# RWKV-7 scan and a four-expert mixture: key and removal vectors turned to channels by loads and VectorE, with one reciprocal of the channel-major decay

## The chip, the cores and the metric

One core of one Trainium2 chip. The metric is the device time of one launch in microseconds: for the kernel before, the median of 3 runs is 1080.28 us (1080.03 to 1081.78). The profiles come from one further execution under the hardware profiler.

## What is computed

A recurrence over 768 steps, for 4 batches and 8 heads with 40 channels each, and behind it a mixture of four two-layer experts on the recurrence's output (3072 rows of 320). All data are fp32.

```python
for t in range(S):                                   # S = 768; state: (B, H, 40, 40)
    y[:, :, t] = einsum('bhd,bhde->bhe', r_t, state)
    Sa = einsum('bhde,bhe->bhd', state, a_t)
    state = state * w_t[:, :, None, :] - einsum('bhd,bhe->bhde', Sa, b_t) + einsum('bhd,bhe->bhde', v_t, k_t)

x = y as (4*768, 8*40);  p = domain_probs / (domain_probs.sum(-1) + 1e-9)
out = sum over e of p[:, e] * (relu(x @ w1[e]) @ w2[e])     # w1: 4 x 320 x 1024, w2: 4 x 1024 x 320
```

The decay w is multiplied up along the steps, per channel. Inside a stretch of steps, the kernel scales k and b by the reciprocal of that running product, and a and r by the product itself; then the stretch is a set of ordinary matrix products.

## The kernel before

**Tiling.** The 768 steps are cut into 12 chunks of L = 64. A chunk of two batches (8 heads each) is a *unit*: 24 units, number u = 2 x chunk + pair of batches. All the work of a unit on the recurrence is in tiles of 128 partitions: either *by tokens* (2 batches x 64 steps on the partitions, 8 heads x 40 channels in the row, 320 elements) or *by channels* (2 heads x 64 places on the partitions, of which 40 carry a channel, 8 pairs x 64 steps in the row, 512 elements).

**One unit on its way.** `within()` (L458) prepares a unit by itself. SP loads the decay in 32-wide pieces as `rawW` (`load_raw`, L264), DVE turns it to channels with two 32x32 stream transposes into G (L475, helper line L286), saves the decay of the last step (gl, L477), sets the first column to zero (G0, L479), and a scan along the row makes the running product (L512; `first` is one in each first column); gl is brought up to the product of all 64 steps (L517). PE turns G back to tokens (pg, L525, four transposes recorded on helper line L113), DVE multiplies by the naturally loaded decay `natW` (gp, L528) and takes the reciprocal of 128x320 (L529). With it DVE makes N = -b/g (n_tok, L556) and K = k/g (k_tok, L561) by tokens, from `natB` and `natK`, and AT from `rawA` (L563, and L565, AG, times G). `VT` and `RT` are the values and receptances by channels, from `rawV` and `rawR`. PE turns N and K to channels (pNT, pKT, `turned()`, L532 to L535), ACT copies them out of PSUM to NT and KT. From these PE makes the scores pc, pfe and pe. POOL then solves a triangular system (`substitute`, Z, L681 and L698), about 22 us a unit; DVE turns the result (Qc, QTc, L709, L710).

`begin_step` is the part that hangs on the state left by the unit two before: prn (PE; with the state), RH (DVE, L760), psat, SX, pxr, RS, then pdy (PE), Y, S+, YG, SG (DVE, L823 to L835). Y, the output, is copied by twelve small SP loads into `xT` (L854), the operand of the mixture.

**The mixture.** For each pair of units and each expert: up-projections `ph` (two PSUM tiles, PE), hs = relu (ACT, L888), five sums of parts of hs on DVE (`a`, L1014), and seven products in the manner of Strassen in place of eight: `p431`, `p75`, `p26` (all shown as `p` in the profile). DVE adds each into the output tile, scaled by the gate (osb: L903, of 320 or of 160 elements). `lead()` lets PE begin the next ph early, before the last matmuls of a scan step. The up-projection weights w1a and w1b come in pieces, three loads each (L365).

**PSUM.** Eight banks: five are handed out in turn under the tag "big" (scan), three under "mm" (ph twice, p431, p75, p26). A bank is given to the next tile only once its last reader is through.

**What sets the order.** PE's order is the program's (`keep_in_program_order`). DVE's is stated in the string VECTOR_ORDER for the first units (the names are `G3.0`, `1/gp3`, ...), with `pin()` beside it for units up to 3; past that the tile scheduler places DVE's instructions by their data and its own costs. SP issues nearly all loads, in one order, which the scheduler makes too; an issue that waits for a tile to come free holds up everything behind it. At most eight of its DMAs are under way at once. Until PADDED = 3 a unit uses other loads; from unit EARLY = 5 on the main loop has its steady order. In the steady state I call *section* s the stretch of about 42.4 us that begins with RH of unit s: it holds the step of unit s and the first half of `within()` of unit s+3.

Of the kernel before, what the change touches and what calls it, by code (L numbers as in the profile page):

```python
# [15 lines left out]

VECTOR_ORDER = """
    Qc1 QTc1 G2.0 G2.1 gl2 G02 scan2 gll2 out1 gp2 1/gp2 N2 K2 AT2 AG2 RTc2.0 RTc2.1 RTc2.2 VTc2.2 blocks2.0
    blocks2.1 M2 M02 Z12 Z22 ET2.0 ET2.1 VC2.0 VC2.1 out2 G3.0 G3.1 gl3 G03 scan3 SX1.1 gll3 SX1.0 VT3 RT3 AT3 AG3
    Y1.1 Y1.0 S+1.0 S+1.1 SG1.0 SG1.1 gp3 1/gp3 N3 K3 out3 VC3.0 VC3.1 Qc2 QTc2 RH2.0 RH2.1 G4.0 G4.1 gl4 G04  # L20
    blocks3.0 blocks3.1 M3 M03 Z13 Z23 ET3.0 ET3.1 out4 SX2.0 SX2.1 scan4 gll4 AT4 AG4 VT4 RT4 Y2.1 Y2.0 S+2.0 YG2
    SG2.0 S+2.1 gp4 SG2.1 1/gp4 N4 K4 out5 VC4.1 VC4.0 sum_w0 Qc3 QTc3 ET4.0 blocks4.0 blocks4.1 ET4.1 M4 M04 Z14
    Z24 RH3.0 RH3.1 G5.0 sum_w1 G5.1 gl5 G05 scan5 gll5 sum_w2 AT5 AG5 out6 SX3.0 SX3.1 sum_w3 VT5 Y3.1 Y3.0 S+3.0
    YG3 SG3.0 S+3.1 gp5 SG3.1 1/gp5 RT5 N5 K5 sum_w4 out7 VC5.1 VC5.0 Qc4 QTc4 ET5.0 blocks5.0 blocks5.1 ET5.1 M5
    M05 Z15 Z25 RH4.0 RH4.1 G6.0 G6.1 gl6 G06 scan6 sum_a4 gll6 sum_w5 sum_w6 AT6 AG6 sum_a0 sum_a1 sum_a2 sum_a3
    SX4.0 SX4.1 sum_w7 VT6 sum_w8 Y4.1 Y4.0 S+4.0 YG4 SG4.0 S+4.1 gp6 SG4.1 1/gp6 RT6 N6 K6 out8 out9 out10 out11
    sum_a5 VC6.1 VC6.0 Qc5 QTc5 out12 out13 ET6.0 blocks6.0 blocks6.1 ET6.1 M6 M06 Z16 Z26 out14 out15 sum_w9 sum_a6
    G7.0 G7.1 gl7 G07 RH5.0 RH5.1 scan7 gll7 sum_a7 sum_a8 sum_a9 AT7 AG7 out16 out17 out18 out19 sum_w10 sum_w11
    SX5.0 SX5.1 sum_w12 sum_w13 sum_w14 sum_a10 sum_a11 out20 sum_a12 out21 sum_a13 VT7 out22 sum_a14 out23 gp7 1/gp7
"""  # L30


# [1 line left out]
def kernel(  # L34
# [42 lines left out]
    P = 128  # L77
# [95 lines left out]
                        base=(2 * j + s) * D - g * P, channel_multiplier=1,  # L173
                    )

    first = const.tile([P, 2 * NJ, L], FP32, name="first")
    nc.gpsimd.memset(first[:], 0.0)
    nc.gpsimd.memset(first[:, :, 0:1], 1.0)


    def kept(name, shape, n, value=0.0, eng=nc.gpsimd, lo=0):
# [19 lines left out]
    for n, a_sum in enumerate(("a1", "a7", "a5", "a2")):  # L201
        t = padded["RV"[n % 2], n // 2] = sb.tile([P, H, 64], FP32, name="padded", tag=a_sum)
        nc.gpsimd.memset(t[:, :, D:64], 0.0)
    raw = {x: kept(f"raw{x}", [P, 2 * NJ, 2 * D], 1, 0.0, nc.vector, D + D - Q) for x in "WARV"}
    k_tok, n_tok = (kept(x, of_64, 2, lo=D) for x in ("k_tok", "n_tok"))

    both = [P, H, D + L]
# [30 lines left out]

    def load(q, names):
        for x in names:  # L240
            q.n[x] = t = sb.tile([P, H, D], FP32, name=f"nat{x}", tag=f"nat{x}", bufs=2 if x in "WV" else 1)
            for i, bb in enumerate(q.b):
                nc.sync.dma_start(
                    out=t[i * L:(i + 1) * L], in_=srcs[x][bb, :, q.c * L:(q.c + 1) * L, :].rearrange("h t e -> t h e"),
                )

    def load_raw(q, names):


        moves = []  # L250
        for x in names:
            q.n["raw" + x] = t = raw[x]()
            heads = srcs[x].rearrange("b h t e -> (b h) t e")[q.b[0] * H:(q.b[1] + 1) * H, q.c * L:(q.c + 1) * L, :]
            heads = heads.rearrange("n (x two) e -> x n (two e)", two=2)
            for r in range(2):
                if x in "RV":

                    sets = ((slice(0, 8, 2), slice(r, 16, 4)), (slice(1, 8, 2), slice(3 - r, 16, 4)))
                else:
                    sets = ((slice(0, 8), slice(r, 16, 2)),)  # L260
                for n, hs in sets:
                    for y, w_ in enumerate((D + Q, 2 * D - Q)):
                        o = slice(64 * r + Q * y, 64 * r + Q * y + Q)
                        moves.append(lambda eng, out=t[o, n, 0:w_], in_=heads[:, hs, Q * y:Q * y + w_]: eng.dma_start(out=out, in_=in_))  # L264
        return moves
# [7 lines left out]
    def part(i):  # L273
        return slice(i * L, (i + 1) * L)
# [119 lines left out]
    def half(s):  # L394
        return slice(64 * s, 64 * s + 64)
# [22 lines left out]
    def tok(x):  # L418
        return lambda j: x[:, 2 * j:2 * j + 2, :].rearrange("p h e -> p (h e)")

    def of_pairs(x, hf, j, i):
        return x[half(hf), j, part(i)]

    def of_slots(x, hf, j, i, n=64):
        return x[64 * hf:64 * hf + n, 4 * i + j, :]
# [36 lines left out]
    def within(q):  # L462
# [3 lines left out]
        def pin(ins, also=False):  # L466
            if q.u <= PADDED or also:
                keep(ins)


        G = sb.tile([P, 2 * NJ * L + 1], FP32, name="G", tag="G", bufs=3)
        q.G = Gv = G[:, 0:2 * NJ * L].rearrange("p (c t) -> p c t", t=L)
        ahead = G[:, 1:2 * NJ * L + 1].rearrange("p (j i t) -> p i j t", i=2, t=L)
        for i in range(2):
            pin(noted(turn_raw(ahead[:, i], n["rawW"][:, NJ * i:NJ * i + NJ, :]), "G", q.u, i), q.u > EARLY + 2)  # L475
        q.gl = sb.tile([P, 2 * NJ, 1], FP32, name="gl", tag="gl", bufs=4)
        ins = nc.vector.tensor_tensor(out=q.gl[:], in0=G[:, L::L][:, :, None], in1=first[:, :, 0:1], op=ALU.mult)  # L477
        pin(noted(ins, "gl", q.u))
        pin(noted(nc.vector.memset(Gv[:, :, 0:1], 0.0), "G0", q.u))  # L479
        q.AT = sb.tile([P, 2 * NJ, L], FP32, name="AT", tag="AT", bufs=2)  # L480

# [24 lines left out]
        if q.u == 1:  # L506
            yield
            VT = turn_rv("V")
            yield
            turn_rv("R")  # L510
            yield
        ins = nc.vector.tensor_tensor_scan(  # L512
            out=G[:, 0:2 * NJ * L], data0=G[:, 0:2 * NJ * L],
            data1=first[:].rearrange("p c i -> p (c i)"), initial=0.0, op0=ALU.mult, op1=ALU.add,
        )
        pin(noted(ins, "scan", q.u))
        ins = nc.vector.tensor_tensor(out=q.gl[:], in0=q.gl[:], in1=Gv[:, :, L - 1:L], op=ALU.mult)  # L517
        noted(ins, "gll", q.u)
        if q.u == 1:
            yield  # L520
        if q.u < 3:
            pin(noted(turn_raw(q.AT[:], n["rawA"][:]), "AT", q.u))
        yield

        pg = turn("pg", tok(Gv), q.u == 2, of_mixture("pg") if q.u == 1 else None)  # L525
        pg = by(pg[:], 64)[:, :, 0:D]
        gp = sb.tile([P, H, D], FP32, name="gp")
        pin(noted(nc.vector.tensor_tensor(out=gp[:], in0=pg, in1=n["W"][:], op=ALU.mult), "gp", q.u))  # L528
        pin(noted(nc.vector.reciprocal(out=gp[:], in_=gp[:]), "1/gp", q.u))  # L529

        yield

        def turned(name, x):
            t = sb.tile([P, NJ, P], FP32, name=name, tag="turned", bufs=3)
            nc.scalar.copy(out=t[:].rearrange("p j t -> p (j t)"), in_=turn("p" + name, tok(x), q.u == 1)[:])  # L535
            return t

        def token_V():
            return n["paddedV"][:, :, 0:D] if q.u < PADDED else n["V"][:]

        def causal_scores(VT):
            pc = quadrants(banks("pc"), 0, BY_TOKENS, L, lambda j, s, i: (
# [6 lines left out]
        def masks(pc):  # L549
# [3 lines left out]
                    pin(ins, q.start)  # L553

        q.K, q.N = k_tok(), n_tok()
        ins = nc.vector.scalar_tensor_tensor(  # L556
            out=q.N[:, :, 0:D], in0=n["B"][:], scalar=-1.0, in1=gp[:], op0=ALU.mult, op1=ALU.mult,
        )
        pin(noted(ins, "N", q.u))
        other = nc.gpsimd if q.u == 1 else nc.vector  # L560
        pin(noted(other.tensor_tensor(out=q.K[:, :, 0:D], in0=n["K"][:], in1=gp[:], op=ALU.mult), "K", q.u))  # L561
        if q.u > 2:
            pin(noted(turn_raw(q.AT[:], n["rawA"][:]), "AT", q.u))  # L563
        at_ij = q.AT[:].rearrange("p (i j) t -> p i j t", i=2)
# [2 lines left out]
        q.VC = VCs()  # L567
        if q.u > 0:
            noted(nc.scalar.copy(out=q.VC[:, :, 0:D], in_=token_V()), "VCv", q.u)
        if q.u >= PADDED:  # L570
            VT = turn_rv()
        yield

        NT = turned("NT", q.N)
        KT = turned("KT", q.K)
        if q.u == 2:
            VT = turn_rv()
        yield
# [1 line left out]
        if q.u == 1 or q.u >= PADDED:  # L580
# [2 lines left out]

        p = banks("pfe")
        pf = quadrants(p, 0, BY_TOKENS, L, lambda j, s, i: (
            s, i ^ s, j, of_slots(q.AT, s, j, i), of_pairs(NT, s, j, i),
        ))
        def copy_F():
            q.F = sb.tile([P, H, L], FP32, name="F", tag="F", bufs=1)
# [6 lines left out]
        if q.apart or q.u == 0:  # L596
            p = banks("pe")
        pe = quadrants(p, NJ * L, BY_TOKENS, L, lambda j, s, i: (
            s, i, j, of_pairs(KT, s, j, i), of_slots(q.AT, s, j, i),
        ))  # L600
        if not q.apart:
            copy_F()
# [139 lines left out]
    def step(q, xT):  # L742
# [85 lines left out]
        if not q.start:  # L828
            noted(nc.vector.tensor_tensor(out=Y[:], in0=Y[:], in1=Gv, op=ALU.mult), "YG", q.u)
        if not q.end:  # L830
            gl = q.gl[:].rearrange("p (j i) o -> p j i o", i=2)
            for i in range(2):
                x = st[i][:, :, 0:D]
                noted(nc.vector.tensor_tensor(out=x, in0=pdy[i][:, :, 0:D], in1=x, op=ALU.add), "S+", q.u, i)
                ins = nc.vector.tensor_tensor(out=x, in0=x, in1=gl[:, :, i, :].to_broadcast([P, NJ, D]), op=ALU.mult)  # L835
                noted(ins, "SG", q.u, i)
# [369 lines left out]
    run(ws[2], 1)  # L1206
    run(s, 2)
    run(ws[2], 1)
    load(units[3], "WBKV")
    run(ws[2], 2)  # L1210
    substitute(units[2], nc.gpsimd)
    mix(1)
# [8 lines left out]
    for u in range(1, NU):  # L1221
# [55 lines left out]

        if u + 3 < NU:
            if u == 1:
                go_now(load_raw(begin(4), "WVRA"))  # L1280
            else:
                go(load_raw(units[u + 3] if ahead else begin(u + 3), "A" if ahead else "WA"))
            load(units[u + 3], "WBKV")
            if u > 1:
                later.extend(load_raw(units[u + 3], "VR"))
        run(w, 2)
# [86 lines left out]
```

## Time and profile before

| what | value |
|---|---|
| median of 3 runs | 1080.28 us |
| profiled execution: span, first to last instruction | 1077.3 us |
| its distance to the median | about 3 us, outside the span |
| granted TensorE clock, mean | 0.998 |
| PE busy in the span | 1062.5 us, 99% |
| DVE, ACT, POOL busy | 758.3, 353.2, 494.3 us |
| chain that ended last, share of PE | 93% (ph 40%, p 31%) |
| DMA: bytes, mean rate | 105.81 MB, 98 GB/s |

A row of a timeline has the start, the duration, the engine, the line, the operation, output<-input, the form, the count of instructions run together, and in brackets the idle time before it with what ended it. A row of a group has its count, then busy time, mean ns of one, and idle time before them. The chain of work that ended last is followed back from the last instruction.

```profile
PE 93%; DVE 3%; DMA 1%; ACT 1%; issue 1%; SPq 0%; POOL 0%; ACTq 0%; DVEq 0%
PE ph L110 40%; PE p L110 31%; PE pdy L110 3%; PE po L110 3%; PE pxr L110 2%; PE psat L110 2%; PE prn L110 2%; PE pfe L110 2%; PE pc L110 1%; PE pev L110 1%; PE pQ L110 1%; PE pe L110 1%; PE pNT L113 1%; PE pg L113 1%; PE pKT L113 1%; PE pY L110 1%
```

### The profile page before, as it was taken

To read this page: it belongs to the slowest core of one execution; us is meant where nothing else is said; L and a number is where in the kernel's file an instruction comes from. 1 tells how busy PE (TensorE), PEld (TensorE's weight loads), DVE (VectorE), ACT (ScalarE), POOL (GpSimd) and SP (SyncE) were. 2 spreads that over 40 slices of the span, in tenths; PEclk is the share of its full clock that TensorE was granted. 3 is DMA by queue.
4 is the path that set the end of the run, shared out by engine and by line. 5 is a ranking of instruction groups with operands and counts; after the bars stand their busy time and mean duration, and the time that the engine had idled before them with its cause. 6 is when DMAs were issued, how large, how long until landed. Compare 5 with 4: busy or idle time off the path is not lost.

```text
span 1077.3 us, 38510 instructions
## 1 busy us (share of the span) xinstructions
PE 1062.5 (99%) x16140; PEld 955.1 (89%) x16140; DVE 758.3 (70%) x1549; ACT 353.2 (33%) x958; POOL 494.3 (46%) x1276
## 2 busy tenths in 40 slices
PE   7999999999999999999999999999999999999998
PEld 7878878899898999999999999999999999998887
DVE  7787679897676776876776768668767776634343
ACT  3433444422432423324333333233243333221110
POOL 5117777747254374363462653733735626520000
PEclk9999999999999999999999999999999999999999
DMA  7776644444444434443353263353343331121220
GB/s 129 192 202 129 142 108 108 101 85 102 103 103 104 104 92 85 115 99 79 91 129 80 59 155 62 83 128 81 90 106 86 96 89 58 54 82 42 84 76 13
DMA packets 258070, 105.81 MB, mean 98 GB/s; under 512 B 212536, under 2 KB 237672, under 8 KB 257896
## 3 DMA queue, kind: packets, MB, share of 16 engines
q1 hardware_dynamic: 253912, 102.51, 40.8%
q8 instruction: 127, 2.08, 0.8%
q10 hardware_dynamic: 3984, 0.84, 0.5%
q14 instruction: 47, 0.39, 0.1%
HBM read 95.40 MB, written 3.93 MB: 92 GB/s over the span
## 4 chain that ended last, share of the span: by engine, by line
PE 93%; DVE 3%; DMA 1%; ACT 1%; issue 1%; SPq 0%; POOL 0%; ACTq 0%; DVEq 0%
PE ph L110 40%; PE p L110 31%; PE pdy L110 3%; PE po L110 3%; PE pxr L110 2%; PE psat L110 2%; PE prn L110 2%; PE pfe L110 2%; PE pc L110 1%; PE pev L110 1%; PE pQ L110 1%; PE pe L110 1%; PE pNT L113 1%; PE pg L113 1%; PE pKT L113 1%; PE pY L110 1%
## 5 line engine op out<-in xcount | busy, mean ns | idle before, releaser
L698 POOL TENSOR_TENSOR Z<-Z 128x31 f32<-128x31 f32 (+7 forms) x704 | 263.8, 375 | 55.2
L1014 DVE TENSOR_TENSOR a<-hs 128x512 f32<-128x512 f32 x220 | 150.7, 703 | 111.6 <-ACT hs L888 111.6
L110 PE MATMUL ph<-xT,w1a 128*128 128x256 f32 (+3 forms) x1536 | 221.3, 374 | 1.7 <-issue 1.7
L888 ACT ACTIVATE hs<-ph 128x512 f32<-128x512 f32 (+1 forms) x208 | 116.9, 564 | 323.5 <-PE ph L110 323.1
L110 PE MATMUL ph<-xT,w1b 128*128 128x256 f32 (+3 forms) x1536 | 222.0, 374 | 0.0
L110 PEld LDWEIGHTS ph<-xT,w1a 128*128 128x128 f32 (+1 forms) x1536 | 167.9, 161 | 30.6 <-issue 9.5
L110 PEld LDWEIGHTS ph<-xT,w1b 128*128 128x128 f32 (+1 forms) x1536 | 168.8, 161 | 26.9 <-issue 6.1
L681 POOL TENSOR_TENSOR Z<-M,Z 128x62 f32<-128x62 f32 (+7 forms) x352 | 142.8, 406 | 98.0 <-DVE M L667 72.1
L110 PE MATMUL p<-sums,a 128*128 128x160 f32 x1056 | 164.9, 299 | 0.0
L903 DVE SCALAR_TENSOR_TENSOR osb<-p,gate,osb 128x320 f32<-128x320 f32 (+1 forms) x243 | 108.1, 481 | 79.2 <-PE p L110 72.9
L110 PEld LDWEIGHTS p<-sums,a 128*128 128x128 f32 x1056 | 152.8, 190 | 2.2
L648 POOL COPY below<-F 32x256 f32<-32x256 f32 x48 | 21.4, 445 | 227.5 <-ACT F L591 225.8
L110 PEld LDWEIGHTS p<-w,hs 128*128 128x128 f32 x704 | 98.6, 190 | 8.5 <-issue 7.3
L110 PE MATMUL p<-w,hs 128*128 128x160 f32 x704 | 104.9, 302 | 0.0
L110 PE MATMUL p<-w,a 128*128 128x160 f32 x704 | 102.8, 299 | 0.0
L110 PEld LDWEIGHTS p<-w,a 128*128 128x128 f32 x704 | 98.0, 190 | 0.0
L716 POOL COPY QT<-QTc 32x256 f32<-32x256 f32 x96 | 40.3, 420 | 71.6 <-DVE QTc L710 65.3
L808 ACT COPY RS<-pxr 64x256 f32<-64x256 f32 x88 | 32.3, 367 | 101.2 <-DVE SX L460 78.8
L629 ACT COPY EV<-pev 64x160 f32<-64x160 f32 x96 | 23.1, 286 | 90.5 <-PE pev L110 90.1
L529 DVE RECIPROCAL gp<-gp 128x320 f32<-128x320 f32 x24 | 51.6, 2152 | 0.7
L651 DVE STREAM_TRANSPOSE M<-blocks 128x1024 f32<-128x1024 f32 x24 | 47.3, 1969 | 2.9 <-ACT blocks L643 2.8
L460 DVE COPY_PREDICATED VC<-mask_up,pc 128x256 f32<-128x256 int32 x48 | 18.7, 443 | 38.4 <-PE pc L110 38.4
(153 smaller groups left out, 1389.4 us busy)
## 6 DMA issues: line engine op xcount, KB each, us to landing
w1a<-in_moe_w_dram SPq DMA_DIRECT2D x37, 512.0 KB
w1b<-in_moe_w_dram SPq DMA_DIRECT2D x37, 512.0 KB
w<-in_moe_w_dram SPq DMA_DIRECT2D x4, 1280.0 KB
w1a<-in_moe_w_dram SPq DMA_DIRECT2D x74, 64.0 KB
w1b<-in_moe_w_dram SPq DMA_DIRECT2D x74, 64.0 KB
natW<-in_w_dram SPq DMA_DIRECT2D x48, 80.0 KB
natB<-in_b_dram SPq DMA_DIRECT2D x48, 80.0 KB
natK<-in_k_dram SPq DMA_DIRECT2D x48, 80.0 KB
```

What stands on the lines that cost most here:

```text
L110: return stated(nc.tensor.matmul(**k))
L113: return stated(nc.tensor.transpose(**k))
L529: pin(noted(nc.vector.reciprocal(out=gp[:], in_=gp[:]), "1/gp", q.u))
L629: nc.scalar.copy(out=of_slot(q.EV[half(p)], i ^ p)[:, :, 0:D], in_=pev[i][half(p)])
L651: ins = nc.vector.transpose(out=M[:], in_=cols)
L681: ins = eng.tensor_tensor(out=Z[:, 1:3, 0:n, j + 1:Q], in0=M[:, j:j + 2, None, j + 1:Q].to_broadcast([P, 2, n, m]), in1=Z[:, here, 0:n, j: ...
L698: eng.tensor_tensor(out=z[:, 0], in0=z[:, 0], in1=z[:, x], op=ALU.add)
L716: ins = nc.gpsimd.tensor_copy(out=q.QT[quarter(i), :, quarter(i % 2)], in_=QTc[quarter(i)])
L808: nc.scalar.copy(out=RS[half(s), x ^ s::2], in_=prs[x][half(s)].rearrange("p (j i) t -> p j i t", i=2),)
L888: ins = nc.scalar.activation(out=h[:, i * HF // 2:(i + 1) * HF // 2, 0:n], in_=ph[i][:], func=ACTF.Relu,)
L903: ins = nc.vector.scalar_tensor_tensor(out=to, in0=p, scalar=sc, in1=to, op0=ALU.mult, op1=ALU.add)
L1014: ins = nc.vector.tensor_tensor(out=t[:], in0=x, in1=y, op=op)
```

## The change

For units 3 to 23 (`by_channel`), G gets one more column, L + 1 in all, so that after the scan its columns 1 to 64 hold the running product with the step's own decay; the scan runs over 520 elements instead of 512. The reciprocal is taken of these columns directly (128x512). K and B are no longer loaded by tokens: they come as `rawB` and `rawK` in 32-wide pieces, eight loads each in place of two, are turned to channels by DVE (BT, KT), and multiplied there by the reciprocal. PE still turns N and K once each, now from channels to tokens, and ACT copies 8x40 elements to n_tok and k_tok. The turn of G on PE (pg), gp, gl, gll and the load natW are gone. AT's matmuls take 40 rows instead of 64 in the products with NT and KT. The tile `first` grows to L + 1, with a copy of the old width for units 0 to 2. rawB and rawK have one buffer, which in the first units serves for the naturally loaded decay, B and K. VECTOR_ORDER loses gl, gll and gp and gains BT and KT from unit 3 on. The core of the diff:

```diff
-    ... G3.0 G3.1 gl3 G03 scan3 SX1.1 gll3 SX1.0 VT3 RT3 AT3 AG3 Y1.1 Y1.0 S+1.0 S+1.1 SG1.0 SG1.1 gp3 1/gp3 N3 K3 ...
+    ... G3.0 G3.1 G03 scan3 SX1.1 SX1.0 VT3 RT3 AT3 AG3 Y1.1 Y1.0 S+1.0 S+1.1 SG1.0 SG1.1 1/gp3 BT3 N3 KT3 K3 ...
...
+                elif x in "BK":
+                    sets = ((slice(0, 8, 2), slice(r, 8, 2)), (slice(1, 8, 2), slice(8 + r, 16, 2)))
                 else:
                     sets = ((slice(0, 8), slice(r, 16, 2)),)
...
+        by_channel = q.u >= PADDED
+        G = sb.tile([P, 2 * NJ, L + 1], FP32, name="G", tag="G", bufs=3)
+        flat = G[:].rearrange("p c t -> p (c t)")
+        if by_channel:
+            q.G = Gv = G[:, :, 0:L]
+            ahead = G[:, :, 1:L + 1].rearrange("p (j i) t -> p i j t", i=2)
...
+        if by_channel:
+            q.gl = G[:, :, L:L + 1]
...
+        decays, starts = (flat, first) if by_channel else (flat[:, 0:2 * NJ * L], first_64)
         ins = nc.vector.tensor_tensor_scan(
-            out=G[:, 0:2 * NJ * L], data0=G[:, 0:2 * NJ * L],
-            data1=first[:].rearrange("p c i -> p (c i)"), initial=0.0, op0=ALU.mult, op1=ALU.add,
+            out=decays, data0=decays, data1=starts[:].rearrange("p c t -> p (c t)"), initial=0.0, op0=ALU.mult,
+            op1=ALU.add,
         )
...
+        gp = sb.tile([P, 2 * NJ, L], FP32, name="gp")
+        if by_channel:
+            pin(noted(nc.vector.reciprocal(out=gp[:], in_=G[:, :, 1:L + 1]), "1/gp", q.u))
+        else:
...
+        def to_tokens(name, x, to):
+            p = turn("p" + name, tok(x))
+            nc.scalar.copy(out=to[:, :, 0:D], in_=by(p[:], 64)[:, :, 0:D])
...
-        if q.u >= PADDED:
+        if by_channel:
             VT = turn_rv()
-        yield
-
-        NT = turned("NT", q.N)
-        KT = turned("KT", q.K)
+            NT = sb.tile([P, 2 * NJ, L], FP32, name="NT", tag="turned", bufs=3)
+            pin(noted(turn_raw(NT[:], n["rawB"][:]), "BT", q.u))
+            ins = nc.vector.scalar_tensor_tensor(
+                out=NT[:], in0=NT[:], scalar=-1.0, in1=gp[:], op0=ALU.mult, op1=ALU.mult,
+            )
+            pin(noted(ins, "N", q.u))
+            KT = sb.tile([P, 2 * NJ, L], FP32, name="KT", tag="turned", bufs=3)
+            pin(noted(turn_raw(KT[:], n["rawK"][:]), "KT", q.u))
+            pin(noted(nc.vector.tensor_tensor(out=KT[:], in0=KT[:], in1=gp[:], op=ALU.mult), "K", q.u))
+        yield
+
+        if by_channel:
+            to_tokens("NT", NT, q.N)
+            to_tokens("KT", KT, q.K)
...
-                go_now(load_raw(begin(4), "WVRA"))
+                go_now(load_raw(begin(4), "WVRABK"))
             else:
-                go(load_raw(units[u + 3] if ahead else begin(u + 3), "A" if ahead else "WA"))
-            load(units[u + 3], "WBKV")
+                go(load_raw(units[u + 3] if ahead else begin(u + 3), "ABK" if ahead else "WABK"))
+            load(units[u + 3], "V")
```

## The prediction, made before the changed kernel had run

> **What bounds the kernel now.** I read the busy shares first, then the span in stretches, then PE's rows beside VectorE's.
>
> ```profile
> span 1077.3 us, 38510 instructions
> PE 1062.5 (99%) x16140; PEld 955.1 (89%) x16140; DVE 758.3 (70%) x1549; ACT 353.2 (33%) x958; POOL 494.3 (46%) x1276
> ```
> ```profile
> 27.00:243.00 216.00, 212.21 (x3777) 181.72 (x3777) 177.44 (x363) 86.23 (x253) 123.78 (x289) 1.00 0.57 133
> 243.00:351.00 108.00, 106.25 (x1674) 96.50 (x1666) 77.61 (x153) 35.89 (x98) 54.91 (x143) 1.00 0.45 103
> 351.00:1060.00 709.00, 709.00 (x10363) 643.56 (x10358) 473.42 (x965) 220.59 (x583) 299.66 (x792) 1.00 0.37 87
> ```
>
> In the stretches the columns are length, then busy time of PE, PEld, DVE, ACT, POOL. From 351 to 1060 us PE has no gap at all. So PE work removed is time won, and any delay of another engine that makes PE stop is time lost, microsecond for microsecond. How near DVE is to that limit is shown by PE's one late stall (first fence PE, second DVE):
>
> ```profile
> 326.13 0.59 PE L110 MATMUL ph<-xT,w1a 64*64 64x256 f32 x2
> 328.47 0.87 PE L110 MATMUL ph<-xT,w1a 64*64 64x256 f32 x11 [1.75 <-issue]
> ```
> ```profile
> 326.80 0.71 DVE L286 STREAM_TRANSPOSE VT<-rawV 128x512 f32<-128x512 f32 x1 [3.50 <-DMA rawV<-in_v_dram]
> 327.44 0.51 DVE L903 SCALAR_TENSOR_TENSOR osb<-p,gate,osb 128x320 f32<-128x320 f32 x1
> 327.98 0.38 DVE L903 SCALAR_TENSOR_TENSOR osb<-p,minus_gate,osb 128x160 f32<-128x160 f32 x1
> ```
>
> VT waited 3.50 us for its load; osb behind it emptied its bank at 328.36, and PE went on 0.11 us later. The label says "issue", but the only late event there is this bank: "mm" has three, in turn for ph and the down products. In a steady unit the same point has slack:
>
> ```profile
> 828.90 0.91 DVE L286 STREAM_TRANSPOSE G<-rawW 128x256 f32<-128x256 f32 x2
> ...
> 830.19 1.22 DVE L512 TENSOR_TENSOR_SCAN G<-G,first 128x512 f32<-128x512 f32 x1
> ...
> 833.53 1.29 DVE L1014 TENSOR_TENSOR a<-hs 128x512 f32<-128x512 f32 x2 [1.31 <-ACT hs L888]
> ...
> 836.15 0.38 DVE L903 SCALAR_TENSOR_TENSOR osb<-p,minus_gate,osb 128x160 f32<-128x160 f32 x1
> ```
> ```profile
> 837.66 1.10 PE L110 MATMUL ph<-xT,w1a 64*64 64x256 f32 x16
> ```
>
> I count from the end of prn's matmuls, 827.9. That osb ends at +8.6 and ph needs the bank at +9.8: **1.0 us of slack** after the 0.11. DVE's only idle before it is 1.31 us.
>
> **The change, part by part.** "Unit" is one of 24, "section" s the stretch that begins with RH of unit s; it prepares unit s+3.
>
> *Removed.* PE's turn of the decay, units 3 to 23:
>
> ```profile
> 814.42 0.60 PE L113 MATMUL pg<-ident,G 128*128 128x128 f32 x4
> 814.95 0.68 PE L110 MATMUL pev<-VC,ET 64*64 64x40 f32 x32
> ```
>
> Start to start 0.53 us; x 21 = **11.1 won**. The turns of N and K stay at their places on PE: the same number of transposes, now from channels to tokens. Their copies out of PSUM stay on ACT (33% busy) and shrink from 512 to 320 elements; I cost that at nothing, since ACT waits for PE and not PE for ACT there, and without that cover it could win or lose 0.1 us a unit. Also gone are gp 0.48 and two gl of 0.18 on DVE. The built order puts VT of section 7 behind other work, so its stall goes: **1.75 won**.
>
> [...]
>
> *Added on DVE per unit.* A reciprocal of 512 elements for one of 320. Before has two rows:
>
> ```profile
> L529 DVE RECIPROCAL gp<-gp 128x320 f32<-128x320 f32 x24 | 51.6, 2152 | 0.7
> L389 DVE RECIPROCAL total<-total 128x24 f32<-128x24 f32 x1 | 0.3, 289 | 0.0
> ```
>
> The slope is (2152-289)/296 = 6.3 ns, so 2.15 + 192 x 6.3 = 3.36 us; bounds 2.15 (no growth) and 2.15 x 1.6 = 3.44. I take **3.4**. Two stream transposes (BT, KT) like AT, 0.70 each; N and K on 512, 0.1 to 0.2 more each. Net 1.25 + 1.40 + 0.34 - 0.84 = +2.2 us of a 42.4 us section in which DVE is 67% busy (473/709). As throughput it is covered; its place is not.
>
> *Moved on DVE* (order of the built program, which holds no times). The reciprocal leaves its place before Y and follows the scan, ahead of AT and of the a's and osb's that free the bank. From section 13 the order is RH, G, scan, RECIP, AT, AG, a, a, osb, a, osb. By the rows above, G starts at +1.0 with AT ahead of RH and at +0.55 without; two G's 0.95, the memset 0.1 and the scan 1.25 end at +2.9, RECIP at +6.3. Then AT, AG and three a's at about 0.62 start to start (3.1), the first osb 0.47 and the second 0.38: +10.2, which is 0.5 past the limit of 9.7 (9.8 less 0.11). The 1.31 us of idle in front of the a's is used up by then. Sections 11 and 14: 0.4. In 8 to 10 and 12, where a's and the osb's stand ahead of part of that: 9.5, nothing. Seven at 0.5 and two at 0.4 make 4.3. Section 5 has two sums and w ahead as well: +11.3, so 1.55. If RECIP doesn't grow at all (2.15), all of this is hidden.
>
> *Moved on SP.* Per unit 16 narrow loads of B and K replace six natural ones. By rows 16 narrow ones took 795.60 to 805.51, 9.9 us (0.43 each, with a longer one about every tenth), in other stretches nearer 9; six natural ones 4.3 to 4.7. So +4.4 to +5.6 a unit, 9 to 11 per 84.4 us from one xT to the next but one, where SP's gaps sum to about 13. The queue nearly closes. The DMA engines themselves are at 0.37 to 0.45 and get about the same bytes, so I cost them at nothing. What a fuller queue moves: in before all four loads of rawW stood ahead of the xT loads of their section. In the order after, the last ones stand behind:
>
> ```profile
> 820.12 9.59 SPq L854 DMA_DIRECT2D xT<-Y  x12
> ```
>
> Since Y no longer waits for the reciprocal (1.3 us earlier), the xT's would end at about -0.1; a narrow load needs 1.9 to 2.1 us from issue to landing in these stretches, so one load behind gives G at about +2.1 instead of its own +0.55: **1.6 late**, 0.5 more for each further load, 4 to 5 behind a w1 piece (1.6 to 1.8 us). All of DVE queues behind G. With slack and RECIP as above: section 8 (a w1 piece between) 4.5; 9 (three loads) 2.4; 10 (behind a w1 piece) 4.3; 11 (two) 2.5; 12 (one) 1.4; 13 (two) 2.6; 14 (one) 2.0; 15, 17, 19 (one) 2.1 each; 16, 18, 20 (none) 0.5 each. **Sum 27.5**, the 4.3 in it. Bounds: 4.3 if the loads land in time; 40 if each lands a us later, as raw loads beside a w1 piece did (3.4 to 4.8 us). I stay with the quiet landings. The w1a piece of even sections is issued near 800.5 for 794.0 and would land at about 805.4, where PE wants it: 0 to 7 over the run, taken 0.
>
> *Early units, PE without slack.* In sections 1 to 4 DVE makes N and K just before PE turns them. In section 1 of before gp starts at 90.61, n_tok ends at 93.96, k_tok at 94.50, and PE turns K at 95.10. After, RECIP starts at 90.6 and takes 3.4; BT, N, KT, K follow at 0.65 to 0.7 each and end at 96.7. PE, which comes 0.5 us earlier for want of pg, would wait for K until 96.8: 1.7 later than before, 2.2 against its own new time. In sections 2 to 4 the same gives 128.5 for 126.3, 160.0 for 157.6, 189.3 for 188.8: 2.9, 3.0, 1.1 with the 0.5 each (the 0.5 is won in the sum above). Together **9.2**. From below 5.4, since PE idles 3.8 us in that stretch already (216.00 less 212.21) and can lose some of it; from above 9.2, as nothing else is moved there. In section 4 the VT and osb's that ran from 218.5 to 220.5, before gp, come behind Y, S+, YG and SG, which wait for pdy (end 219.9); about 4.3 us later the bank would be free, at 224.3 where p<-w,hs wants it at 220.8: 3.5. RT comes late too, and pc waits 0.45.
>
> *Sum.* -11.1-1.75+9.2+3.95+1.55+27.5 = **+29.4**: span 1106.7, time 1109.7 from the median 1080.28, which is 3 us above this span (lead and tail outside it, kept). I say 1109.
>
> [...]
>
> **Rivals.**
> *A, faster.* DVE's lateness from unit 7 on costs PE nothing: "issue" at 328.47 was no bank, or hs (idle 1.31) and not DVE sets the chain. Then all terms that go by the bank fall (27.5, 3.95, 1.55), and of the early 9.2 about half stays, as a late pKT is partly caught up at PE's next wait: -12.9+4.6 = -8.3, near 1072. Its place is ph of each section; apart from the label it also decides wherever G starts by +0.6 and RECIP takes under 2.9 us, which is 0.5 less than I take. For it speaks the label; against it, that PE went on 0.11 us after the bank, the usual distance from a DVE end to PE.
> *B, smaller loss.* The last rawW loads land before G is due, because xT starts still earlier or its twelve issues are shorter (8.9 to 9.6 us by the rows; they would have to be 1.6 shorter). The loss is 29.4 less 23.2 (27.5 less the 4.3 of RECIP): +6, 1086.
> *C, SP closes.* The 13 us of gaps are used up (they are not spread evenly: 7.7 of them lie in one piece before the w1b loads at 852.69), w1 pieces come late by the 7 above, and some rawW loads land like those beside a w1 piece (3 more): 1119. For it: 9 to 11 of 13; against: the queue's one long gap stands just where the new loads go.
> That the turn isn't removed is excluded: the built PE order has 21 groups of four less and nothing new.
>
> **How the numbers follow.** Forecast 0.49 (1100 to 1116), A 0.16 (1066 to 1078), B 0.18 (1080 to 1099), C 0.13, and 0.04 that losses of early units and the gain cancel (within 0.2%, about what a measurement of this kernel can tell). Faster 0.16, same 0.04, slower 0.80. The range 1078 to 1122 leaves out A and the end of C.
>
> **What would show it.** Right: gaps of PE at ph about 9.8 us after prn, each 0.11 us behind an osb; DVE's G waiting on DMA rawW for 1.5 to 2.5 us in sections 8 to 15, 17, 19; pKT waiting on DVE between 95 and 190 us; RECIP at 3.4. Wrong: G without a wait (B), PE without gaps after 350 us (A), PE waiting on w1a or w1b (C).

## The result, and the profile after

The changed kernel takes 1141.74 us (median of 4, 1133.89 to 1143.51) against 1080.80 for the kernel before (median of 4, 1080.03 to 1081.78): a ratio of 1.0551 with a 95% interval of 1.0517 to 1.0586. The forecast of 1109 had the sign and the place, and half of the size; the time lies outside the range of 1078 to 1122. One correction first: section s begins with RH of unit s+1, not of unit s as the chapter on the kernel and the prediction say; the rows and the s+3 of the prediction are as meant.

The profiled execution has a span of 1140.7 us, 63.4 more than before. From the page of the changed kernel:

```profile
span 1140.7 us, 38541 instructions
PE 1080.5 (95%) x16056; PEld 961.8 (84%) x16056; DVE 805.2 (71%) x1528; ACT 348.3 (31%) x958; POOL 508.0 (45%) x1280
...
PEclk9999989999999899989999999999999999999999
```

PE has 84 matmuls fewer, as it should, and yet is busy 18 us longer: it ran slower for part of the time (the row PEclk shows 8s, before had only 9s; the mean granted clock is 0.979 for 0.998). The same three stretches as in the prediction, with PE's busy time in the second column and the granted clock third from the end:

```profile
27.00:243.00 216.00, 200.19 (x3444) 168.76 (x3444) 173.06 (x329) 78.66 (x234) 119.23 (x285) 0.97 0.54 131
243.00:351.00 108.00, 107.52 (x1688) 97.78 (x1687) 88.37 (x158) 37.90 (x106) 48.63 (x124) 1.00 0.39 86
351.00:1060.00 709.00, 673.91 (x10126) 606.67 (x10126) 490.51 (x924) 213.01 (x580) 323.80 (x816) 0.98 0.36 85
```

The last stretch, which had no gap, now has 35 us of gaps. PE's waits by what ended them (total, times, longest):

```profile
PE ph L111 <- issue: 34.6, 14, 6.5
PE p L111 <- DVE osb L962: 3.5, 1, 3.5
PE pNT L114 <- DVE NT L620: 3.5, 2, 2.1
PE pKT L114 <- DVE KT L626: 3.1, 4, 0.9
```

All four rows are places that the prediction names: ph at the bank, p in section 4, and the turns of N and K in the early units. By the ends of prn, section 8 starts 13.2 us later than before (374.34 for 361.10), sections 8 to 20 take 50.2 us longer (601.76 for 551.61), and the rest takes what it took. Of the 13.2, 2.5 lie ahead of section 1 (104.93 for 102.42 at the end of the first prn). That part need not come from the change: in e5 below, which is the kernel before up to section 8, the same point lies at 105.15.

One section shows the chain. Section 15, prn's end at 705.40; SP, then DVE, then PE:

```profile
696.33 9.40 SPq L913 DMA_DIRECT2D xT<-Y  x12
705.78 0.48 SPq L288 DMA_DIRECT2D rawW<-in_w_dram  x1
```
```profile
708.47 0.77 DVE L310 STREAM_TRANSPOSE G<-rawW 128x256 f32<-128x256 f32 x2 [2.38 <-DMA rawW<-in_w_dram]
...
710.55 3.35 DVE L564 RECIPROCAL gp<-G 128x512 f32<-128x512 f32 x1
...
717.58 0.37 DVE L962 SCALAR_TENSOR_TENSOR osb<-p,minus_gate,osb 128x160 f32<-128x160 f32 x1
```
```profile
718.06 1.55 PE L111 MATMUL ph<-xT,w1a 64*64 64x256 f32 x11 [2.29 <-issue]
```

One load of rawW stands behind the twelve xT loads. G waits for it, RECIP follows, and the osb that frees the bank ends at 717.95, 12.6 after prn, where ph wanted the bank at 9.8. PE goes on 0.11 us later, as it did in the kernel before.

### The profile page after: what moved, and what is told of

The parts are those of the page before. It is cut to its first block, busy times and chain, and to the rows that moved or that the text cites. A ratio compares the mean times of both kernels' runs of the same rounds, so it can differ in the third digit from the quotient of the medians.

```text
span 1140.7 us, 38541 instructions
## 1 busy us (share of the span) xinstructions
PE 1080.5 (95%) x16056; PEld 961.8 (84%) x16056; DVE 805.2 (71%) x1528; ACT 348.3 (31%) x958; POOL 508.0 (45%) x1280
## 4 chain that ended last, share of the span: by engine, by line
PE 83%; issue 4%; DVE 4%; SPq 3%; DMA 3%; ACT 1%; POOL 1%; DVEq 0%; POOLq 0%; ACTq 0%
PE ph L111 37%; PE p L111 28%; PE pdy L111 3%; PE psat L111 2%; SPq L288 2%; PE pxr L111 2%; PE prn L111 2%; DMA w1b<-in_moe_w_dram 1%; PE pfe L111 1%; PE pc L111 1%; PE po L111 1%; PE pev L111 1%; PE pQ L111 1%; PE pKT L114 1%; PE pe L111 1%
## 5 line engine op out<-in xcount | busy, mean ns | idle before, releaser
L757 POOL TENSOR_TENSOR Z<-Z 128x31 f32<-128x31 f32 (+7 forms) x704 | 259.6, 369 | 55.2
L111 PE MATMUL ph<-xT,w1a 128*128 128x256 f32 (+3 forms) x1536 | 231.9, 386 | 19.7 <-issue 19.7
L111 PE MATMUL ph<-xT,w1b 128*128 128x256 f32 (+3 forms) x1536 | 228.7, 378 | 15.6 <-issue 14.9
L111 PEld LDWEIGHTS ph<-xT,w1a 128*128 128x128 f32 (+1 forms) x1536 | 172.7, 166 | 53.3 <-issue 31.4
L740 POOL TENSOR_TENSOR Z<-M,Z 128x62 f32<-128x62 f32 (+7 forms) x352 | 152.2, 432 | 143.4 <-DVE M L726 117.6
L111 PEld LDWEIGHTS ph<-xT,w1b 128*128 128x128 f32 (+1 forms) x1536 | 171.3, 163 | 46.5 <-issue 23.9
L1073 DVE TENSOR_TENSOR a<-hs 128x512 f32<-128x512 f32 x220 | 154.1, 718 | 47.8 <-ACT hs L947 47.8
L707 POOL COPY below<-F 32x256 f32<-32x256 f32 x48 | 25.2, 524 | 219.0 <-ACT F L650 217.4
L564 DVE RECIPROCAL gp<-G 128x512 f32<-128x512 f32 x21 | 70.3, 3350 | 0.5
L310 DVE STREAM_TRANSPOSE G<-rawW 128x256 f32<-128x256 f32 x48 | 18.5, 421 | 36.5 <-DMA rawW<-in_w_dram 27.3
```

What stands on the lines that cost most here:

```text
L111: return stated(nc.tensor.matmul(**k))
L564: pin(noted(nc.vector.reciprocal(out=gp[:], in_=G[:, :, 1:L + 1]), "1/gp", q.u))
L707: tc.keep_in_program_order(nc.gpsimd.tensor_copy(out=q.below[quarter(i)], in_=q.F[quarter(i), :, 0:Q]))
L740: ins = eng.tensor_tensor(out=Z[:, 1:3, 0:n, j + 1:Q], in0=M[:, j:j + 2, None, j + 1:Q].to_broadcast([P, 2, n, m]), in1=Z[:, here, 0:n, j: ...
L757: eng.tensor_tensor(out=z[:, 0], in0=z[:, 0], in1=z[:, x], op=ALU.add)
L1073: ins = nc.vector.tensor_tensor(out=t[:], in0=x, in1=y, op=op)
```

## The experiments

**Theory 1**: DVE is late for the bank, because loads stand behind xT on SP and RECIP stands ahead of the osb's; a long stop of PE then costs clock as well. **Rival 1**: SP is too full, whatever the order. **Rival 2**: RECIP alone. **Rival 3**: "issue" is no bank. Where no count is given, a time is that of one run; the kernel before took 1079.74 to 1083.66 us in the 13 runs beside e5 to e8.

**e1: rawW ahead of xT.**

```diff
-        ahead = u + 3 < NU and u in range(EARLY, EARLY + 3)
+        ahead = EARLY <= u < NU - 3
```

> The changed kernel, with one word of the program different: the loads of rawW for the unit three ahead are asked for at the head of a section in every section, not only in the first three steady ones, so that all four stand ahead of the xT loads. rawA still stands behind them. Theory (place of the loads): most of the 57 us that sections 8 to 20 lose goes. G no longer waits; what is left is AT's wait of about 1.3 us for rawA plus 0.5 for the reciprocal ahead of the bank, as sections 16, 18 and 20 of the changed kernel have it (1.7 us lost each at a gap of 1.0): 8 sections at 1.7, 5 at 0.5 or less, about 16 in all, so near 1101 us, with the granted clock back to 0.99 or more. Rival (the queue is too full, whatever its order): the w1 pieces are late in place of rawW, PE waits for DMA, and the time stays at 1125 to 1142.

Measured: 1094.26, beside 1080.92 of before; clock 0.994. One line takes 47 of the 61 us away. From section 5 on G waits for no load (+0.6 everywhere), and PE's row for ph shrinks to:

```profile
PE ph L111 <- issue: 2.7, 4, 1.0
```

Three of the four are in sections 14, 16 and 18, where AT still waits for rawA, as foreseen; in 13, 15, 17 and 19 the osb ends at +9.9, 0.2 past the limit, no gap shows, and the section is 0.2 longer (42.19 us for 41.98 where nothing is late). Theory 1 holds, and rival 1 falls as the cause of the 47.

**e2: rawA ahead as well.** In this kernel AT of a unit is made from the A of the next one, because the tile is filled again before it is read; so part of its data, and the order of its waits, aren't those of the changed kernel.

```diff
-            go(load_raw(begin(u + 3), "W"))
+            go(load_raw(begin(u + 3), "WA"))
```

> The changed kernel with rawW and rawA both asked for at the head of every section; rawB and rawK come last. In the order that results DVE makes AT in the second half of the section, and only the reciprocal stands ahead of the a's and osb's. Theory (place of the loads): no stop of PE at ph from section 8 on, since the second osb ends at about +9.0, under the limit of 9.7; left are the early sections, which cost 13 net up to section 8, and the gain of 0.53 a section: 1142 less 57 = about 1085, clock 0.99. Rival (queue too full): w1 pieces or rawK late, 1110 or more. Second rival (the reciprocal itself holds the bank): gaps of 0.5 and more in every section, 1095 or more.

Measured: 1125.84. The osb's come in time in most sections (+8.64), but PE now stops at pY, and in two sections still at ph:

```profile
PE pY L111 <- DVE QTc L769: 12.8, 7, 3.3
PE ph L111 <- issue: 6.6, 3, 3.4
```

VT and BT moved ahead of M on DVE, and VT waits for its load, 1.4 to 4.5 us ahead of each stop at pY of over 1 us; POOL's Z starts later, and Qc and QTc behind it. In sections 17 and 19 VT, waiting 4.0 and 4.4 us, stands ahead of the osb's, and ph stops for 2.9 and 3.4. A miss, useful for this alone: an engine whose order is scheduled gives a stop another place when one load moves.

**e3: rawB and rawK on ScalarE's queue.**

```diff
+                go(load_raw(units[u + 3], "BK"), nc.scalar)
```

> The changed kernel with the sixteen loads of rawB and rawK of each unit from 5 on issued by ScalarE's queue and not by SP's; nothing else is changed in the program, and with the relieved queue the scheduler puts rawW and rawA a section ahead, as in the kernel before. Theory (SP had no room, so the scheduler set the loads late): no wait of G or AT; base loss 0.5 a section from AT ahead of the a's at most; ACT spends about 7 us a unit on issuing at 31% busy, which may delay hs by a load's 0.5 us here and there: 1083 to 1095. Rival (issuing costs ACT more than SP): hs late by 2 us or more each unit, PE stops at p or ph in every section, 1110 or more. If the order alone matters, e2 and e3 end alike.

Measured: 1116.82, the rival's number at another place. Sections 8 to 20 take 551.09 us for 551.61 before, without a wait of G, so the steady part is near the theory; but the start of section 8 lies at 399.5, 25 later than in the changed kernel. In the early sections ACT stands in PE's chain: eight rawK issues take it 8.9 us, and PE waits 3.9 us for the hs behind them. Many small waits follow, and the clock lost ahead of section 8 is 17.1 us for 5.1 in the changed kernel.

**e4: RECIP behind M, loads left late.**

```diff
+    behind_m = [(f"Z2{k - 1}", f"1/gp{k}") for k in range(8, NU)]
```

> The changed kernel with the reciprocal of units 8 and up put behind the building of M (and so behind the a's and the first osb's) on VectorE; the loads stay late. Theory (late loads and the reciprocal add up ahead of the bank): every wait ahead of the bank shrinks by 3.35 us. Sections 9, 11 to 20 lose nothing, 8 and 10 keep a gap of about 3, section 5 none: 1142 less 57 plus 10 plus less 1 = about 1094. Rival (G's late load alone sets the stop, the reciprocal is hidden behind hs): gaps of 8 to 20 stay, 1130 or more. Second rival: the reciprocal now delays the four osb's of p431 and PE waits there instead, 1110 or more.

Measured: 1109.14, between theory and rival. ph stops 10.5 us in all for 34.6:

```profile
PE ph L111 <- issue: 10.5, 6, 2.9
```

The osb's come 3.3 to 3.7 us earlier in sections 8 to 11, 13 and 19 (section 8: +13.18 for +16.72, section 10: +12.65 for +16.34), about RECIP's length, and 0.4 to 2.8 earlier in 12, 14, 15, 17 and 20; G's wait stays. 16 and 18 don't gain (+12.50 and +12.00), because there the next in line, AT, waits for rawA. So late load and RECIP add up, and RECIP alone (rival 2) isn't it: in e1 it stands in its place and PE hardly stops. The second rival of the forecast comes near in number (1110 or more), but PE's one wait at p for an osb is the 3.4 us of section 4, which the changed kernel has too.

**e5: idle work ahead of G, in the kernel before.**

```diff
+        for k in range(LATE.get(q.u, 0)):
+            ins = nc.vector.memset(G[:], 1.0)
+            keep(ins)
```

> The kernel before, with nothing but idle work added on VectorE: in sections 8 to 20 the turn of the decay stands behind 3, 5, 7, 9, 11, 14, 3, 5, 7, 9, 11, 14 and 4 memsets of G (each an estimated 0.51 us from the 128x256 memset of 0.27 and the 128x128 one of 0.165), so G comes 1.6 to 7.3 us late, 54 us in all. Theory (late DVE passes to PE through the bank behind its 1.0 us of slack, and a long stop of PE then costs the clock as well): sections with a delay under 2 lose the delay less 1.0; the longer ones lose that and 1 to 3 us more, with the granted clock at 0.5 for some microseconds after a gap of more than 2 to 3 us. 41 from the delays plus 10 to 18 from the clock: 1131 to 1139. Rival (the clock in the changed kernel falls for another reason, not for the stop): 41 alone, 1121, and a clock of 0.998. Second rival (PE's label 'issue' is no bank): under 1090.

Measured: 1094.31, a miss. In sections with a long delay the scheduler put a's and osb's ahead of the memsets, so G came up to 11 us after prn and the osb's at +9.7 to +10.3. What it does show: in section 9 G comes at +4.32 (before +1.01), the osb ends at +10.22, and the section takes 42.94 for 42.41. The rule "osb's end plus 0.11 less 9.79" gives 0.54 lost; 0.53 are. Sections 10 and 11 agree as well: 0.64 and 0.48 by the rule, 0.63 and 0.48 measured. Here work was added on DVE alone, so rival 3 falls. The osb of section 9, whose prn ends at 406.00:

```profile
415.84 0.37 DVE L909 SCALAR_TENSOR_TENSOR osb<-p,minus_gate,osb 128x160 f32<-128x160 f32 x1
```

It leaves the clock untested except by one gap of 2.58 us (from 835.85), after which 1.71 us of clock were lost.

**e6: the kernel before without pg** from unit 3 on (gp is made from the natural decay alone, so N and K have other values).

```diff
+        if q.u < PADDED:
+            pg = turn("pg", tok(Gv), q.u == 2, of_mixture("pg") if q.u == 1 else None)
+            pg = by(pg[:], 64)[:, :, 0:D]
+        else:
+            pg = n["W"][:]
```

> The kernel before without the turn of the decay on PE for units 3 and up: gp is made from the natural decay alone, so that N and K have other values; all other work is kept. Theory (PE is the bound, start to start 0.53 us each): 21 x 0.53 = 11.1 less, 1069.5, perhaps 1 to 2 more since the stall of section 7 hangs on a late load. Rival (PE's time is refilled by its other waits): less than 5 won, 1076 or more.

Measured: 1077.70 beside 1081.78. Sections 8 to 20 take 545.93 for 551.61: **0.44 us a section**, not 0.53, with PE busy without a gap:

```profile
351.00:1060.00 709.00, 709.00 (x10436) 643.33 (x10436) 479.99 (x969) 223.21 (x590) 306.51 (x796) 1.00 0.36 88
```

The rest of the expected 11 was lost before section 8, which starts 2.8 us late: 1.5 of it ahead of section 1, where runs differ anyway, and 2.1 in one stop at ph in section 6 (other sections win some back). There the order put gp and RECIP ahead of the osb's, and gp waits for its load:

```profile
283.98 0.49 DVE L531 TENSOR_TENSOR gp<-natW 128x320 f32<-128x320 f32 x1 [4.32 <-DMA natW<-in_w_dram]
```

It is the chain of the changed kernel again (late load, DVE, bank, ph), in a kernel without rawB and rawK.

**e7: e1, and units 3 to 6 by tokens as before.**

```diff
-        by_channel = q.u >= PADDED
+        by_channel = q.u >= BY_CHANNEL      # 7
...
+ ("out23", "Y5.0"), ("out23", "Y5.1")      # section 4: osb's ahead of Y again
```

> As e1 (rawW ahead), and in addition units 3 to 6 by tokens as in the kernel before (with its order of VectorE up to there, and VT of unit 7 and its osb's put ahead of Y again): the change from unit 7 on only. Theory (the early loss comes from N and K that PE waits for, and in section 4 from the late osb's): the start of section 8, at 374.4 in e1 and 361.1 in before, goes back to 358 to 360 and the rest is as in e1: 1094.3 less 15 = 1079, within 3. Rival (the early loss comes from the sixteen loads of raw B and K, which stay from unit 7 on, or is shifted to later): 1086 or more.

Measured: 1085.03. Section 8 starts at 363.56 for 374.40 in e1: 10.8 of the early loss is the early units' N and K and section 4's late osb's. Of the 6 us missing to the forecast some 4 lie before section 8, 3.0 of them in sections 4 (PE waits 0.9 for K of unit 7 and 1.5 for RT) and 5 (ph 0.6), and 1.8 behind it, where AT waits for rawA in other sections than in e1.

**e8: e7, and AT behind the osb's.**

```diff
+    moved += [(45 + 16 * (k - 9), f"AT{k}") for k in range(11, NU)]
```

> As e7, and in addition AT of unit 11 and up is put behind the osb's of the first bank on VectorE, so that neither the late rawA nor AT itself stands ahead of the bank. Theory: the gaps of 0.7 to 1.0 in sections 12 to 18 of e1 go, PE runs from 350 us on without a gap, each section is 0.53 shorter than before: 1080.9 less 0.53 x 17 = 9 less 1.75 plus 1 to 3 for sections 4 and 5: 1071 to 1074. Rival (pfe then waits for the late AT, or the queue is late with w1 pieces): 1078 or more.

Measured: 1083.83 (10 runs), ratio 1.0024 (1.0006 to 1.0042) to before. Every osb is at +8.64 from section 8 on, so no bank is late; and the time is the rival's. What came up in its place:

```profile
PE ph L110 <- DMA w1b<-in_moe_w_dram: 3.7, 3, 2.2
```

Weights come late, up to 2.2 us, and waits of 0.3 to 1.1 follow at p. So rival 1 is next in line once the order is mended; e10 tries that.

**e9: half the loads, nothing else.** rawB and rawK in four loads each, as W and A, and two half transposes for one.

```diff
-                elif x in "BK":
-                    sets = ((slice(0, 8, 2), slice(r, 8, 2)), (slice(1, 8, 2), slice(8 + r, 16, 2)))
...
-            pin(noted(turn_raw(NT[:], n["rawB"][:]), "BT", q.u))
+            for i in range(2):
+                to = NT[:].rearrange("p (j i) t -> p i j t", i=2)[:, i]
+                pin(noted(turn_raw(to, n["rawB"][:, NJ * i:NJ * i + NJ, :]), "BT" if i else "Bh", q.u))
```

> The changed kernel with rawB and rawK loaded in four loads each in place of eight (the arrangement that rawW and rawA have), and turned by two half transposes each, which costs VectorE an estimated 0.4 us a unit (two of 0.44 for one of 0.70). The built order of SP is that of the changed kernel, with the last loads of rawW and all of rawA behind the xT loads in the same sections, but the queue has about 4 us less to issue in every unit. Theory (the place of the loads, which Y and the xT loads fix): G still waits 1.2 to 7 us, PE still stops in sections 8 to 20, 1120 to 1145. Rival (the fullness of the queue): the waits go with the 4 us, 1105 or less.

Measured: 1148.81, with the order of the loads unchanged:

```profile
PE ph L111 <- issue: 41.2, 14, 7.6
```

This is a little above the theory's range. With eight issues fewer in each unit the stops add up to more, 41 us for 35. From section 8 to 19 SP issues for 32.7 us a section here, for 36.2 in the changed kernel and 32.6 in the kernel before: the queue is as free as it was before the change, and G waits up to 8.7 us all the same. Place and fullness are told apart: place is what costs here.

**e10: e8 with the loads of e9.**

> As e8 (rawW ahead, AT behind the osb's, units 3 to 6 the old way), with the four loads each for rawB and rawK of e9. Theory (what is left in e8 from section 8 on, 9 us above the 545.9 of thirteen sections at 42.42 less 0.44, is the full queue: w1b late by 0.5 to 2.2, and what follows it): these waits go, 1083.8 less 6 to 9 = 1075 to 1078, so faster than the kernel before by 3 to 6. Rival (the waits for w1b come from where the pieces stand in the order, or the 0.4 us more on VectorE shows): 1081 or more.

Measured: **1074.88** (4 runs, 1073.18 to 1076.17) beside 1082.27 of before (7 runs), ratio 0.9925 (0.9901 to 0.9949), clock 1.00 in the profiled run. Sections 8 to 20 take 546.05 us, where e6's gain alone gives 545.9, and PE's row is full again, while DVE has 34 us more than before:

```profile
351.00:1060.00 709.00, 709.00 (x10372) 642.87 (x10364) 507.70 (x979) 219.28 (x586) 306.19 (x794) 1.00 0.37 88
```

This version beats both kernels, the kernel before by 0.75%. The idea pays 0.44 us a unit; the changed kernel lost it by where its loads stood.

## The clock

After 6.46 us without work in section 8 of the changed kernel (PE stops at 384.71):

```profile
384.00:387.00 3.00, 0.71 (x23) 0.25 (x14) 2.97 (x2) 1.45 (x4) 1.19 (x3) 0.94 0.29 48
387.00:390.00 3.00, 0.00 (x0) 0.00 (x0) 3.00 (x5) 0.00 (x0) 0.00 (x0) 0.50 0.37 66
390.00:393.00 3.00, 1.83 (x20) 1.25 (x24) 3.00 (x7) 0.00 (x0) 0.00 (x0) 0.50 0.49 82
393.00:396.00 3.00, 3.00 (x68) 2.74 (x63) 2.88 (x5) 1.12 (x5) 0.00 (x0) 0.50 0.89 237
396.00:399.00 3.00, 3.00 (x13) 2.56 (x13) 1.61 (x4) 1.16 (x3) 0.86 (x4) 0.86 0.36 68
```

At 1.9 us into the gap the granted clock falls to 0.50, and it stays there 5.7 us after PE has work again. In all these traces, between start-up and end, the clock lost comes in steps: 1.71, 3.41 or 5.12 us of full clock, that is 3.4, 6.8 or 10.2 us at half. From section 8 on, where PE works without other gaps, no gap under 2.2 us lost any; of the eleven from 2.2 to 2.7 (in the changed kernel, e2, e4, e5 and e9) six did; all from 2.9 up did. In the early sections, where several short gaps lie close together, it also fell after 1.29 us (e2, from 238.00) and 1.07 us (e3, from 217.16). In the changed kernel 2.29 us was enough in sections 15 and 16, and 2.69 us in section 9 was not, so these runs give no one length that decides. Its four runs spread by 9.6 us at clocks of 0.979 to 0.985; no run here shows that the clock is the cause of this spread.

## Why the prediction was wrong

*Right.* The bound (PE), the sign, the bank of "mm" as the way by which DVE's lateness reaches PE, and the four places. RECIP at 128x512 took 3.35 for 3.4, by the slope of two rows. The formula for the stop held: osb end plus 0.11 less 9.79 gives 1.67 in section 18, and its length is 1.71 over the 41.98 of an undisturbed one; in sections 9, 14, 17 and 20, the others without lost clock or a late weight, it agrees within 0.1.

*The step that failed is "Sum 27.5" for sections 8 to 20: the mechanism held, its inputs were too small.* With the osb ends of the changed kernel's trace the same formula gives 42 (section 8: 7.0, 10: 6.7, 11: 3.8, 19: 3.6, 9: 3.3, 13: 3.1, 15 and 16: 2.9, 12: 2.1, 14: 1.9, 18: 1.7, 17 and 20: 1.6). Two inputs were off:
- "xT's would end at about -0.1" and "1.9 to 2.1 from issue to landing". xT ends at -0.2 to +1.7, and behind it a load of rawW landed after 2.0 to 2.8 us, after 4.0 to 4.1 beside a w1 piece. G came at +1.9 to +3.6 with one load behind (+2.1 forecast) and at +8.2 and +7.8 in sections 8 and 10. The prediction had the 4 us landings as an upper bound and took the quiet ones.
- rawA was left out. It stands behind the xT loads too, and in sections 16, 18 and 20, priced at 0.5 each, AT waits for it. In section 18 the row names rawB, but AT reads rawA alone, whose last load landed 0.2 us before AT starts:

```profile
849.05 0.71 DVE L310 STREAM_TRANSPOSE AT<-rawA 128x512 f32<-128x512 f32 x1 [1.30 <-DMA rawB<-in_b_dram]
```

RECIP's own share was forecast too high: in e1, where no load is late for G, the osb's of sections 13, 15, 17 and 19 end 0.2 us past the limit and not 0.5.

*A term that was missing: the clock.* The formula's 42, with about 1 us for a late w1b in section 12, is 43; sections 8 to 20 lost 50.2 and the 5.7 of gain that was eaten, 55.9 in all. The remaining 13 are PE at half clock: 17.1 us of clock were lost there, 13.5 of them while PE worked. It shows section by section: 8, 10, 11, 13, 15, 16 and 19, in which the clock fell, are 1.4 to 2.7 us longer than the formula says, and the others without a late weight 0.0 to 0.1.

*Early units.* Before section 8, 3.4 and 1.7 us of clock were lost after the stops at 162 and 232 us, the latter partly in its gap. With them the forecast of +8.7 at section 8 (9.2 + 3.95 + 1.55 - 1.75 - 8 x 0.53) comes near the 13.2 measured, but partly by luck: 2.5 of the 13.2 lie ahead of section 1, and PE waited 6.6 us for N and K, not 9.2 (in section 3 for 0.7 and not 3.0). The 9.2 is also 0.3 too much by its own figures: 2.2 + 0.5 and 2.4 + 0.5 are 2.7 and 2.9. The 3.5 for section 4 was right (3.52).

*Term by term, sections 8 to 20*: forecast 27.5 less 6.9 = +20.6; measured +50.2. Of the 29.6 between them about 15 are late data, 13 clock, and 1.2 the gain that is 0.44 and not 0.53: start to start of pg was more than PE gets back.

*Rivals.* A fell: PE has gaps. B fell: G waited for rawW in each of the ten sections for which the prediction has a load behind xT. C was wrong for the changed kernel (w1b late once, 0.8 us), and by e9 not its cause; but it is what stops PE in e8, as soon as the order is right. Its price was too high as well: the new loads take SP 7.4 us a unit where the old ones took 4.0, so 3.4 more and not 4.4 to 5.6; the 9.9 us for 16 loads from 795.60 on are a slow stretch, the mean for V and R in sections 8 to 19 is 8.1.

*Left open.* Why the scheduler put rawW and rawA behind xT. Taking the sixteen loads off SP brought them forward (e3), halving them did not (e9), although SP then issues no longer than before the change. So the fullness that the traces show doesn't decide it by itself; what the scheduler reckons with, no run here shows.

## What to carry to other kernels

When a bound engine has 1 us of slack at a buffer, look for the load that the engine in front of it waits for, and price every load that the new order puts behind a late block of issues, all inputs of the section and not only the first; take the landing times seen beside large transfers (here 4.0 to 4.1 us for rawW and not 2.0 to 2.8). Price a stop of PE as long as those after which the clock fell here (from 2.29 us on, in the steady part) at its length and up to the 2.7 us of slower work seen behind it, and spread the range accordingly. And before dropping an idea that came out slower, state the order of its loads: here four edits, to the place of one load, to one instruction's place, to the packing and to the first units, turned 5.5% slower into 0.75% faster.

## What the runs showed of the hardware

From section 8 on, half clock came in pieces of 3.4 us at 0.50, one to three of them for gaps of 2.29 to 7.63 us (changed kernel, e2, e4, e5, e9). Four 128x128 fp32 transposes on PE, whose first started 0.53 us ahead of the next work, gave back 0.44 us when they went (e6; 0.43 in e10). A 128x512 reciprocal on DVE took 3350 ns (changed kernel) and a 128x320 one 2152 (before): 6.2 ns for each of the 192 further elements of a row.
